# Sums of the last three output tiles of a first convolution on TensorE, 64-column sums of the input, and a new instruction order

## The chip, the cores and the metric

The kernel runs on one core of one Trainium2 chip. Time is device time in microseconds (us) for one execution; the figure to compare is the median of several executions. A profiled execution has a time of its own, and its trace spans a little less than that time.

A core has five engines that run their own instruction streams in order and wait for each other with semaphores: TensorE (PE; its weight loads are listed as PEld), VectorE (DVE), ScalarE (ACT), GpSimd (POOL) and SyncE (SP). Transfers are issued from the SP and POOL queues here.

## The reference

The input is x with 2 images of 512 channels of 64 x 64 pixels. Both convolutions are 3 x 3 with 512 output channels; group norm has 4 groups of 128 channels.

```python
h = conv3(_silu(gn(x, g1, be1)), w1)
emb = _silu(t_emb) @ w_emb
h = h + emb.reshape(B, C, 1, 1)
h = conv3(_silu(gn(h, g2, be2)), w2)
return x + h
```

The second norm needs the sum and the sum of squares of h over each group of 128 channels, which is one tile of partitions. The kernel sums the convolution's output without the embedding, and adds the embedding's part by arithmetic; a matmul with a constant matrix (line 319) then sums over the 128 partitions.

## The kernel before

**Tiling.** A chunk is half an image, 32 rows, so there are four chunks; an output tile is 128 channels of a chunk. A layer has 16 groups (chunk by output tile), numbered 0 to 15; groups 0 to 7 are image 0. The convolution uses a transform over rows, four rows to a tile, with six products ("positions"). Positions 0 and 5 are direct matmuls of 512 columns into single banks `acc` (line 934), two of which exist. The four middle positions are partly nested once more over columns and use 256-column matmuls into two-bank tiles `nst` (line 942) or `mid` (line 934).

**Inputs of the matmuls.** `activate` (line 627) applies norm and SiLU on ScalarE to one channel tile of a chunk, into `ak`; `transform` (lines 641 to 678) and `columns` (lines 558 and 563) make the planes V on VectorE. Weights R arrive by DMA and become matrices U on VectorE and ScalarE (lines 309, 308, 421, 394), in part with an accumulating transfer from the POOL queue (line 432).

**Outputs.** TensorE's banks are copied with a factor (`evac`, printed as line 308 on ScalarE or 309 on VectorE), combined on VectorE (lines 987 to 1008) and written to a ring of five buffers: three hold results `yst`, two hold a second addend `z`. For layer 0 `fin` issues an accumulating DMA from the POOL queue (line 1069) that adds z to y, and then the store of y to `h_scr` (line 1073). After that, with the next group, `sum_up` runs two passes over y on ScalarE with an accumulated output (line 795): Identity for the sum, Square for the sum of squares. `gn2_me` (lines 507 to 519) turns these into mean and mean square, and `gn2_scale` into the second norm's scale and bias.

**Sums of x.** For the first image `stats0`, for the second `gn1_stats`, use matmuls with 128 x 128 blocks of x (channels by pixels) as weights and a column of ones (`sums_pe`, line 367). Such a matmul sums over the channels and leaves 128 pixel places, over which the blocks accumulate; since the norm's group is the whole tile, the total over places is all that is needed. `gram_pe` (line 362) has the block on both sides, and its diagonal holds sums of squares.

**Order.** A table `ORDER` lists for each engine the order of its instructions, and `in_order` imposes it. `FLIP` is a string with a digit for each scaled copy, 394 in all, and says whether the copy goes to the other engine than its default (ScalarE for evacuations, VectorE for the rest).

Of the kernel before, what the change touches and what calls it, by code (L numbers as in the profile page):

```python
# [10 lines left out]
ALU = mybir.AluOpType  # L11
# [53 lines left out]
0-31 90-122 32-43 123 44-56 124 156 125 157-162 126 163-172 127-136 173-181 137-153 182-187 154-155 57-73 188 74-79  # L65
189-252 80-89 254 286 255 287-317 256-258 253 320-335 259-277 336-351 278-285 318 358 370-385 359-360 352-353
386-401 354-355 319 356-357 364-369 408-410 420-423 402-403 424-435 361-362 414 404-407 415-419 363 411-413 458 461
436-451 459 452-453 460 462-463 454 464-465 455 466 470-485 467 456-457 468-469 486-501 511-512 508 502-503 509
514-519 504-507 510 513 520-525 544-549 526-533 550 534-536 551 537 552-553 538-542 592-593 543 554-559 568 560-565
580 566-567 569-570 581-583 571-572 594 573-575 595 576 584-585 596-600 586-589 601-608 624-625 590-591 626-634 609  # L70
635-638 577-579 639-644 610-621 645 648 622-623 646-647 649-654 673 661 674 655-659 675 660 662-670 689 705-716 671
717-721 672 722-725 676 726-728 677-678 690-701 737 702-703 738 704 679-680 749-750 681-687 751-752 688 753-760
739-744 729-730 745 761 731-736 762 746 763 777 747-748 778-779 793-815 780-786 825-826 787-789 816 827 790-792 837
828 764-776 829-835 838 836 839-848 817 849 865 850-851 818 852 819-822 866-867 853-857 823 868-869 824 870-871 858
872 859 873 860-864 874-879 881 880 882-903 905-907 904 913 908 914-915 925 909 916 926 910-912 937-938 917 927-928
939-940 918 929-931 919 953 941-945 954 920 932 946 921 947-949 922 955-957 950 969 923 951-952 924 958 933-936
959-966 970-974 967-968 975 1001 976-978 1002-1004 1013 979-992 1005 1014-1015 993 1006 1016-1018 994 1025-1026
1019-1022 1027 1023 1028-1030 1007 1024 1031-1032 995-1000 1033-1036 1008-1009 1037-1038 1010-1011 1039-1040 1012
1041 1057-1058 1042 1059-1060 1043 1061 1044-1048 1062-1063 1049-1050 1064-1065 1051-1054 1066-1075 1055-1056
1076-1087 1109 1088 1097 1089 1110-1111 1090-1091 1112-1120 1125-1132 1092-1093 1141 1133 1142 1134-1136 1094 1137  # L80
1095 1138-1140 1098-1099 1121-1124 1100 1096 1101-1108 1143-1147 1157-1172 1148-1156 1173-1181 1185-1193 1182-1183
1194 1184 1195-1209 1213 1210-1212 1214-1242 1245-1260 1243 1261-1262 1285-1291 1263-1264 1244 1265-1267 1301-1302
1268-1284 1303-1315 1317-1319 1292 1316 1320-1327 1293-1295 1328-1332 1296-1300 1349-1353 1361-1362 1354-1357
1333-1348 1363 1358-1359 1373-1381 1360 1364 1382-1386 1365-1367 1387-1389 1405 1390-1394 1368-1371 1395-1404 1372
1406-1429 1437 1430-1431 1438-1441 1432-1436 1442-1443 1450-1451 1444-1448 1452-1459 1462-1463 1460-1461 1464
1478-1493 1449 1494-1495 1465-1477 1496-1502 1526-1528 1538 1529-1531 1539-1541 1510-1518 1542 1503-1509 1543
1519-1525 1532-1537 1544-1551 1566-1581 1552-1565 1582-1614 1626-1627 1615-1619 1628-1631 1638-1639 1620-1624 1632
1625 1633-1636 1654-1661 1637 1662-1670 1640-1653 1671-1701 1726-1730 1702 1731 1703 1732-1737 1704-1705 1714-1716
1706-1710 1717-1719 1711-1713 1720-1725 1742-1744 1738-1741 1745-1746 1758 1747-1749 1759-1760 1750-1757 1761-1770
1774-1777 1790-1798 1778-1785 1799 1802 1814 1771 1786-1787 1772-1773 1800 1803-1804 1788-1789 1805 1815-1816  # L90
1806-1809 1801 1810-1813 1830 1846 1831 1847 1832 1848-1853 1833 1854-1861 1834-1835 1862-1864 1817-1829 1865-1869
1836-1845 1894-1909 1870-1874 1882 1910-1912 1883-1891 1913 1926-1928 1875-1881 1929-1930 1914-1918 1892 1931-1940
1893 1919 1941-1951 1920-1925 1952-1961 1974-1985 1962-1963 1990-1992 1964 1993 1965-1967 2006-2007 1968-1969 2008
1994 2009-2012 1995-2000 1970-1971 2001-2005 2013-2015 1972-1973 2016-2025 2030-2033 2026-2028 2034-2035 1986 2036
2042-2045 2037 2046 2029 2047 1987 2048 1988-1989 2049 2038-2039 2050-2053 2040-2041 2054 2070-2071 2086 2055-2056
2087-2088 2057-2059 2089 2060-2064 2090 2072 2091 2065-2069 2073-2075 2092 2076-2077 2093 2078-2085 2094-2101 2110
2102 2111-2113 2103-2105 2123 2114 2124-2131 2115 2106-2109 2116-2117 2135-2136 2132 2137-2140 2151 2141-2145 2133
2118 2146 2167 2152 2119 2147-2149 2153 2120 2150 2134 2154-2156 2121-2122 2157-2159 2168-2171 2160-2164 2172
2165-2166 2173-2178 2183-2198 2179-2181 2199 2182 2200-2201 2211 2202-2205 2212 2223 2206-2208 2224-2226 2239-2241
2227-2231 2255-2258 2232 2259 2213 2260-2263 2242-2243 2214-2217 2209-2210 2218-2219 2244 2220-2222 2245 2233-2236  # L100
2246 2237-2238 2247-2252 2264 2253-2254 2265-2270 2287-2289 2271-2286 2290-2294 2299-2300 2311-2321 2327 2322
2328-2339 2301 2323-2326 2340-2342 2302-2303 2343-2344 2304 2295 2345 2296-2298 2305-2307 2346 2308-2310 2347-2354
2359-2372 2355-2356 2373 2357-2358 2374 2399-2414 2375-2377 2387-2396 2378-2380 2415-2421 2381-2382 2422-2423
2383-2384 2424-2426 2385-2386 2427-2430 2397-2398 2431-2446 2463-2464 2447-2462 2465-2471 2475 2487 2476 2488-2489
2477-2481 2503-2504 2482-2486 2505 2519-2521 2472-2474 2506-2509 2522-2525 2490-2502 2526 2510-2516 2527-2528
2517-2518 2529-2534 2551-2556 2535-2550 2557-2563 2575-2583 2591 2584 2564-2566 2607 2585-2587 2592 2588-2590 2608
2593 2567 2594 2568-2574 2609-2611 2595-2606 2612-2620 2623-2625 2639 2626-2628 2621-2622 2629 2640-2641 2663
2630-2631 2664-2665 2632-2635 2651 2636-2638 2666-2667 2652 2642 2668 2643-2644 2669 2653-2654 2670 2645-2646
2671-2672 2647-2648 2673-2677 2655 2678-2679 2656-2659 2680 2660 2681 2695 2682 2661 2683-2685 2662 2686-2690
2696-2701 2691-2694 2702-2704 2649-2650 2705-2726 2751-2764 2727-2728 2739 2765-2766 2740 2729-2733 2741-2742  # L110
2734-2737 2743 2767-2769 2744 2738 2770-2772 2783-2784 2773-2777 2745 2778 2746 2779-2780 2747-2748 2785-2786
# [76 lines left out]
def kernel(  # L188
# [1038 lines left out]
```

## Time and profile before

| | |
|---|---|
| median of 3 runs | 460.18 us (459.57 to 462.43) |
| profiled execution | 459.88 us |
| its span in the trace | 457.9 us |
| TensorE busy | 444.0 us (97%), 3238 matmuls |
| VectorE busy | 431.3 us (94%) |
| ScalarE busy | 386.6 us (84%) |
| GpSimd busy | 75.6 us (17%) |
| passes for sums, line 795 | 32 of 1918 ns, 61.4 us |
| one-column sums, line 367 | 224 matmuls |
| accumulating DMA, line 1069 | 28 of 512 KB, median 4.7 us from issue to landing |

Busy time of TensorE is modelled for matmuls that overlap, so the distance between starts says more than the duration of one. A wait is named by the engine whose semaphore ended it. Layer 0 ends and layer 1 begins near 220 us; some of layer 1's input work is done ahead of that.

### The profile page before, as it was taken

What the parts mean: (1) busy time and instruction counts of PE and PEld (TensorE: products, weight loads), DVE (VectorE), ACT (ScalarE), POOL (GpSimd) and SP (SyncE); (2) the same over time, 40 slices, a digit from 0 to 9 for tenths busy, and PEclk for the clock granted to TensorE, in tenths of its full rate; (3) what the DMA queues carried; (4) which work ended last, traced back from release to release, by engine and by line L of the source; (5) the groups of instructions that cost most, each with busy time, mean ns of one, the idle gap of its engine ahead of it and who ended that gap; (6) DMA issues with size and microseconds to landing.
All of it is one profiled execution on the core that took longest, in us unless ns stands there. A gap on an engine that the chain in (4) does not pass through costs nothing.

```text
span 457.9 us, 8441 instructions
## 1 busy us (share of the span) xinstructions
PE 444.0 (97%) x3238; PEld 288.2 (63%) x3238; DVE 431.3 (94%) x828; ACT 386.6 (84%) x423; POOL 75.6 (17%) x119
## 2 busy tenths in 40 slices
PE   7999999999999999997999999999999999999996
PEld 7844454556555667665656645557666666668874
DVE  2999999999999999999999999998999989999796
ACT  5899999979998798789999999647878696969761
POOL 1223301021000001210121211113221221211110
PEclk9989999999999999999899999999999999999999
DMA  8999765543846462447879895466967769637565
GB/s 311 358 385 235 155 172 146 164 129 103 190 130 159 99 180 66 120 141 212 226 164 263 217 208 125 107 139 165 211 149 184 179 163 206 137 93 151 127 155 169
DMA packets 25011, 80.05 MB, mean 175 GB/s; under 512 B 2827, under 2 KB 6027, under 8 KB 24587
## 3 DMA queue, kind: packets, MB, share of 16 engines
q0 software_dynamic: 10080, 34.87, 37.3%
q1 hardware_dynamic: 14832, 44.64, 29.4%
q8 instruction: 25, 0.41, 0.3%
q14 instruction: 15, 0.12, 0.1%
q10 hardware_dynamic: 59, 0.01, 0.0%
HBM read 42.54 MB, written 16.78 MB: 130 GB/s over the span
## 4 chain that ended last, share of the span: by engine, by line
PE 60%; DVE 19%; ACT 8%; DMA 6%; issue 6%; POOL 2%; DVEq 0%; ACTq 0%; POOLq 0%
PE nst L942 23%; PE acc L934 21%; PE mid L934 13%; ACT rm L308 2%; DVE ak L641 2%; DVE V L678 2%; ACT ak L627 2%; PE acc L1037 2%; DMA g1t<-in_w_dram 1%; DVE V L558 1%; ACT ring L795 1%; DMA out_dram<-ring 1%; DMA ring<-in_x_dram 1%; ACT ring L308 1%; PE half L934 1%
## 5 line engine op out<-in xcount | busy, mean ns | idle before, releaser
L942 PE MATMUL nst<-V,U 128*128 128x256 f16 x1600 | 210.2, 273 | 3.7 <-DVE rm L309 2.4
L942 PEld LDWEIGHTS <-U 128*128 128x128 f16 x1600 | 154.3, 97 | 55.3 <-issue 5.0
L934 PE MATMUL acc<-V,R 128*128 128x512 f16 x696 | 182.6, 384 | 1.3 <-DVE V L661 0.8
L934 PEld LDWEIGHTS <-R 128*128 128x128 bf16 x744 | 71.5, 97 | 63.5 <-issue 1.8
L308 ACT ACTIVATE rm<-nst 128x1024 f16<-128x1024 f32 x98 | 97.8, 1025 | 10.5 <-PE nst L942 4.9
L934 PE MATMUL mid<-V,U 128*128 128x512 f16 x336 | 85.3, 385 | 0.7 <-DVE U L421 0.7
L795 ACT ACTIVATE ring<-ring 128x2048 f16<-128x2048 f16 x32 | 61.4, 1918 | 1.1 <-ACT rm L308 0.7
L627 ACT ACTIVATE ak<-ak,nb_all,sc_all 128x2112 f16<-128x2112 f16 (+1 forms) x28 | 60.2, 2156 | 2.3 <-DVE nb_all L526 2.3
L934 PEld LDWEIGHTS <-U 128*128 128x128 f16 x336 | 32.4, 97 | 36.2 <-DVE U L421 1.4
L308 ACT ACTIVATE ring<-ring 128x512 f16<-128x512 f16 x58 | 35.0, 627 | 23.3 <-DVE ring L1001 16.4
L1069 POOL DMA_DIRECT2D ring<-ring x28 | 26.5, 946 | 143.6 <-ACT ring L308 122.5
L308 ACT ACTIVATE ak<-ak 128x520 f16<-128x520 f16 (+1 forms) x34 | 38.2, 1142 | 3.0 <-DVE ak L648 2.9
L641 DVE TENSOR_TENSOR ak<-ak 128x2080 f16<-128x2080 f16 x32 | 39.4, 1232 | 0.1
L678 DVE TENSOR_TENSOR V<-ak 128x1040 f16<-128x1040 f16 x54 | 38.2, 707 | 0.7 <-ACT ak L308 0.5
L989 DVE TENSOR_TENSOR rm<-tu,rm 128x1024 f16<-128x1024 f16 x50 | 34.1, 682 | 1.0 <-ACT rm L308 0.8
L563 DVE TENSOR_TENSOR V<-V 128x512 f16<-128x512 f16 (+1 forms) x62 | 34.1, 555 | 0.0
L308 ACT ACTIVATE ring<-acc 128x512 f16<-128x512 f32 x52 | 29.6, 596 | 1.8 <-DVE ring L309 0.8
L558 DVE TENSOR_TENSOR V<-V 128x1024 f16<-128x1024 f16 (+1 forms) x31 | 30.2, 978 | 0.2 <-PE acc L934 0.2
L421 DVE TENSOR_TENSOR U<-U,g1t 128x1536 f16<-128x1536 f16 x32 | 30.1, 945 | 0.0
L988 DVE TENSOR_TENSOR tu<-rm 128x512 f16<-128x512 f16 x50 | 20.8, 415 | 2.6 <-ACT rm L308 2.5
L648 DVE TENSOR_TENSOR ak<-ak 128x1040 f16<-128x1040 f16 x32 | 22.5, 702 | 0.1
L668 DVE TENSOR_TENSOR V<-ak 128x1040 f16<-128x1040 f16 x32 | 22.3, 697 | 0.0
(132 smaller groups left out, 444.9 us busy)
## 6 DMA issues: line engine op xcount, KB each, us to landing
ring<-ring POOLq DMA_DIRECT2D x28, 512.0 KB, 4.7
ak<-h_scr SPq DMA_DIRECT2D x16, 528.0 KB, 3.7
h_scr<-ring SPq DMA_DIRECT2D x16, 512.0 KB, 3.7
ring<-in_x_dram POOLq DMA_DIRECT2D x14, 512.0 KB, 5.6
out_dram<-ring POOLq DMA_DIRECT2D x14, 512.0 KB, 5.1
ak<-in_x_dram SPq DMA_DIRECT2D x12, 528.0 KB, 4.5
R<-in_w_dram SPq DMA_DIRECT2D x16, 384.0 KB, 5.2
U<-U POOLq DMA_DIRECT2D x14, 384.0 KB, 5.6
```

The lines of the kernel that those rows point to most:

```text
L308: return nc.scalar.activation(out=o, in_=i, func=ACT.Copy, scale=f)
L421: nc.vector.tensor_tensor(out=o, in0=i0, in1=i1, op=op)
L558: nc.vector.tensor_tensor(out=lo2.rearrange("p c q (t w) -> p (q t) c w", w=HALF), in0=plane_pair(0, HALF + 2), in1=plane_pair(1, HALF), o ...
L563: nc.vector.tensor_tensor(out=hi2[:, c].rearrange("p q (t w) -> p (q t) w", w=HALF), in0=i0, in1=i1, op=op)
L627: nc.scalar.activation(out=at[:, lo - r0:hi - r0, 1:W + 1], in_=sap, func=ACT.Silu, bias=nb_all[:, layer, b, ct:ct + 1], scale=sc_all[:, l ...
L641: nc.vector.tensor_tensor(out=diff, in0=diff, in1=below, op=ALU.add)
L678: nc.vector.tensor_tensor(out=o, in0=in0, in1=in1, op=op)
L795: behind(nc.scalar.activation(out=junk, in_=y, func=func, scale=scale, accum_out=acc), inst)
L934: nc.tensor.matmul(out, lhsT=w_direct(pos, ct, kx), rhs=rhs, start=first, stop=last)
L942: nc.tensor.matmul(accs["nst", (pos - 1) // 2][bank][:, q, :, plane, :], lhsT=lhsT, rhs=rhs.rearrange("p (t w) -> p t w", w=HALF), start=s ...
L989: nc.vector.tensor_tensor(out=msl[:, 1 - k:4 - k:2].rearrange("p q t w -> p q (t w)"), in0=tu[:].rearrange("p q t e w -> p q (t e w)"), in ...
L1069: add_z = lambda: nc.gpsimd.dma_start(out=flat(yst), in_=ring[:, NY + turn % NZ], accum_op=ALU.add)
```

## The change

Three parts:

- For groups 13, 14 and 15 of layer 0 the plain sums are made on TensorE. `weighted_sums` takes the 16 blocks of 128 columns of y as weights, with three columns on the other side: ones, the embedding of the second image in bf16, and what bf16 leaves of it. The result, for 128 pixel places, is the sum over channels of y and of y times the embedding; it goes into an `acc` bank and is copied to `sum_pe` by VectorE. The Identity pass of these three tiles is left out; the Square pass stays. `gn2_me` adds the weighted sums for the second image.
- `sums_pe` writes as many columns of ones as its output has: 64 for channel tiles 1 to 3 of image 0 and channel tile 0 of image 1, one for the others. One of the equal columns is read.
- All five tables of `ORDER` and the string `FLIP` are replaced. Five copies for U and one evacuation go from VectorE to ScalarE, and nine copies within the ring the other way; many others change places.

`D_BY_DMA` is false for every tile in both kernels, so the lines under it run in neither.

```diff
+    SUM_BY_PE = lambda grp: grp >= 13
...
-    FLIP = "0100100011000000000000100010010100000110...
+    FLIP = "1001101011010000000011000110000100010001...
...
-            nc.tensor.matmul(sm, lhsT=blk, rhs=ones_bf[:], start=(j == 0), stop=(j == len(blocks) - 1))
+            nc.tensor.matmul(sm, lhsT=blk, rhs=ones_bf[:].broadcast_to([P, sm.shape[1]]),
+                             start=(j == 0), stop=(j == len(blocks) - 1))
...
-        b1 = b0[:, P:P + 1]
+        b1 = b0[:, P:P + (P // 2 if ct == 0 else 1)]
...
+    def emb_columns():
+        nc.vector.memset(ones_emb[:, :, 0], 1.0)
+        nc.vector.memset(sum_pe, 0.0)
+        nc.vector.tensor_copy(out=ones_emb[:, :, 1], in_=emb_sb[:, :, B - 1])
+        nc.vector.tensor_tensor(out=ones_emb[:, :, 2], in0=emb_sb[:, :, B - 1], in1=ones_emb[:, :, 1], op=ALU.subtract)
+
+    def weighted_sums(y, ot):
+        acc = ps_acc.tile([P, NFREE], F32, tag="acc", name="sm")
+        n = y.shape[1] // P
+        for j in range(n):
+            nc.tensor.matmul(acc[:, 0:3], lhsT=y[:, j * P:(j + 1) * P], rhs=ones_emb[:, ot], start=(j == 0), stop=(j == n - 1))
+        nc.vector.tensor_copy(out=sum_pe[:, ot], in_=acc[:, 0:3])
...
+        if b == B - 1:
+            nc.vector.tensor_tensor(out=m0[:, 0], in0=sum_pe[:, :, 1], in1=sum_pe[:, :, 2], op=ALU.add)
+            for k, (part, scale) in enumerate(((sum_pe[:, :, 0], 1.0 / HW), (m0[:, 0], 2.0 / HW))):
+                nc.vector.scalar_tensor_tensor(out=me[:, k], in0=part, scalar=scale, in1=me[:, k], op0=ALU.mult, op1=ALU.add)
...
-            sums_pe(pcs, b1[:, 0:1])
+            sums_pe(pcs, b1[:, 0:P // 2])
...
-            y, junk, s1, s2 = to_sum.pop()
-            for func, scale, acc in ((ACT.Identity, 1.0, s1), (ACT.Square, float(HW) ** -0.5, s2)):
+            y, junk, s1, s2, ot = to_sum.pop()
+            if ot is not None:
+                nc.vector.memset(s1, 0.0)
+                weighted_sums(y, ot)
+            for func, scale, acc in ((ACT.Identity, 1.0, s1), (ACT.Square, float(HW) ** -0.5, s2))[ot is not None:]:
...
+                if (layer, grp) == (0, 10):
+                    emb_columns()
```

More of the change, by code (lines that the diff above doesn't have):

```diff
@@ L285 @@
         nc.gpsimd.memset(ak[:, 0:AROWS * WP].rearrange("p (r w) -> p r w", w=WP)[:, :, 0:1], 0.0)
-    gparm = consts.tile([4 * CT, P], BF16, name="gparm")
+    gp_all = consts.tile([P, P], BF16, name="gp_all")
+    gparm = gp_all[0:4 * CT]
     tparm = consts.tile([B * ET, P], BF16, name="tparm")
@@ L742, in stats0 @@
             ps_g = b1.bitcast(BF16)[:, 0:4 * CT]
-            nc.tensor.transpose(ps_g, gparm[:], ident[:4 * CT, :4 * CT])
+            nc.tensor.transpose(ps_g, gparm, ident[:4 * CT, :4 * CT])
             nc.vector.tensor_copy(out=gb[:], in_=ps_g)
@@ L1054, in ends_close, with close_group @@
                         nc.vector.tensor_tensor(out=y4[:, 0:4:3], in0=t5, in1=tt[:], op=ALU.add)
-                def close_group(layer=layer, b=b, ch=ch, ot=ot, rows=rows, turn=turn, yst=yst, y4=y4, tt=tt,
+                def close_group(layer=layer, b=b, ch=ch, ot=ot, grp=grp, rows=rows, turn=turn, yst=yst, y4=y4, tt=tt,
                                 accs=accs, by_dma=by_dma, zt=zt, by_z=by_z, ends=ends, ends_close=ends_close):
```

213 lines of the change are left out of this document (107 added, 106 removed), and 4 rows, old and new, of the table ORDER.

## The prediction

> **What bounds the kernel now.** I read the page first: busy times by slice, then the waits of TensorE.
>
> ```profile
> PE   7999999999999999997999999999999999999996
> DVE  2999999999999999999999999998999989999796
> ACT  5899999979998798789999999647878696969761
> PEclk9989999999999999999899999999999999999999
> ```
>
> ```profile
> PE nst L942 <- DVE rm L309: 2.4, 1, 2.4
> ...
> PE nst L942 <- ACT rm L308: 1.2, 3, 0.8
> ```
>
> The first four are the page's slices (40 of 11.4 us; tenths busy, and the granted clock), the last two rows of TensorE's waits (us in total, times, longest). TensorE is full but for the start, the end and one place near slice 19 (206 to 230 us), the change of layers. There VectorE and ScalarE are full too, and the clock digit falls to 8, as it does in slice 3. The table by stretches (length, then busy time and count for PE, PEld, DVE, ACT and POOL, granted clock, DMA) shows both falls:
>
> ```profile
> 18.90:22.31 3.41, 2.90 (x81) 2.72 (x78) 3.41 (x10) 3.41 (x3) 0.10 (x1) 1.00 0.99 386
> 22.31:25.72 3.41, 3.40 (x40) 2.03 (x37) 3.41 (x9) 3.41 (x6) 0.94 (x2) 0.50 0.98 325
> 25.72:47.00 21.28, 20.17 (x163) 9.85 (x161) 20.84 (x51) 20.77 (x19) 5.59 (x7) 1.00 0.98 302
> ...
> 213.46:216.87 3.41, 1.05 (x11) 0.78 (x9) 3.41 (x7) 3.41 (x4) 0.71 (x1) 1.00 0.65 115
> 216.87:220.28 3.41, 3.41 (x17) 2.43 (x17) 3.41 (x7) 2.60 (x5) 1.27 (x2) 0.50 0.61 197
> ...
> 233.00:290.00 57.00, 57.00 (x342) 32.80 (x340) 56.70 (x107) 56.01 (x61) 11.06 (x15) 1.00 0.83 195
> ```
>
> At half clock 3.41 us of matmuls cost 1.7 us more. The timelines of TensorE and of ScalarE (start, busy time, and in brackets the idle time before and who ended it) show the place closely. TensorE waits 2.36 us for an evacuation on VectorE, then 0.80 us for one on ScalarE that stands behind the two 1.9 us passes of an earlier tile's sums:
>
> ```profile
> 209.05 5.42 PE L942 MATMUL nst<-V,U 128*128 128x256 f16 x48
> 216.83 3.57 PE L942 MATMUL nst<-V,U 128*128 128x256 f16 x16 [2.36 <-DVE rm L309]
> ...
> 231.78 2.46 PE L942 MATMUL nst<-V,U 128*128 128x256 f16 x21 [0.80 <-ACT rm L308]
> ```
>
> ```profile
> 224.30 1.91 ACT L795 ACTIVATE ring<-ring 128x2048 f16<-128x2048 f16 x1
> ...
> 226.72 1.90 ACT L795 ACTIVATE ring<-ring 128x2048 f16<-128x2048 f16 x1
> ...
> 230.72 1.92 ACT L308 ACTIVATE rm<-nst 128x1024 f16<-128x1024 f32 x2
> ```
>
> **A measure.** Starts follow each other at 25 ns (1 column), 56 (128), 110 (256) and 221.5 (512) in undisturbed runs of matmuls. Pricing every matmul so gives 436.6 us of clean time: 1600 x 0.1104 + 1032 x 0.2215 = 405.2, and 31.4 for the rest. Call lag the start of a matmul less the clean time ahead of it. The last matmul ends at 453.7, so the lag ends at 17.1. It is 10.4 at the U wait before 47.02, still about 10.4 at 200, 11.3 at 201.21, and 16.3 at 231.78; only 0.8 comes later. After the last matmul 4.1 us go to the last sums and stores, and 2.0 lie around the span: 436.6 + 17.1 + 4.1 + 2.0 = 459.8, the profiled execution being 459.88. The median of the three runs is 460.18, 0.3 above it.
>
> **The change, part by part.** Added TensorE work: 48 matmuls of 3 columns, at the 25 to 27 ns of 1 and 2 columns, make 1.2 us. 128 sums go from 1 to 64 columns. No row has 64; between 25 ns and 56 ns lie +0 and +4.0 us in all. I take 28 ns, half of the 56 ns of 128 columns, since 128 to 512 columns scale so: +0.5 (3 ns x 128 = 0.4, a little more for starts). Clean time becomes 438.3, +1.7; this is paid whole wherever TensorE sets the end, which is nearly everywhere after 233.
>
> Removed: three ScalarE passes, 1.9 us each, 5.7 in all. Their passes stand now between 243 and 271 (L795 rows at 243.38, 251.25 and 266.80 begin the pairs). TensorE waits for nothing there: the row 233 to 290 has it busy 57.00 of 57.00. So by themselves they give the path nothing; they only make room after the crowded place.
>
> Front: the half clock at 22.31 follows a stretch with 63 one-column matmuls of 25 ns, in which the array streams next to nothing, and waits of 0.7 us. With 64 columns it streams nearly always, so I expect no fall there: 1.7 us on TensorE. But VectorE is busy 20.84 of the next 21.28 us, and the U that ends the wait before 47.02 is its work. In the new order VectorE has 1.8 us less before that U, and TensorE 0.8 less clean time: lag 9.4, against 10.4. ScalarE has 5 to 8 us more copies there (copies moved to it); the evacuation before clean 38.9 then ends near 48.7 to 49.5, a lag of 9.8 to 10.5. I take 10.0.
>
> Of the replaced choices, nine copies of ring rows go to VectorE (0.20 for 0.48 us) and five of U to ScalarE (0.73 for 0.27): in all ScalarE's work falls from 372.7 to 367.3 us, VectorE's stays at 423.
>
> New order at the change of layers. I count the work queued ahead of what TensorE waits for, with starts at 0.90 (rm), 0.48 (ring), 2.04 (activation L627), 1.89 (L795), 0.53 (ak), 1.37 and 0.73 (U) us. Before: from the first activation of layer 1 (196.28) to the evacuation that frees 231.78 stand 32.9 us of ScalarE work and 1.3 of waits. After: 30.7, since one activation and two copies of U and g1t are moved behind it; 1.0 of waits. The first activation itself needs the scale of layer 1, and VectorE now has 2.7 us more ahead of that chain, which waits for POOL's power (2.04 us) in between: 196.3 to 197.5, I take 197.0. ScalarE then frees TensorE at 197.0 + 30.7 + 1.0 + 0.9 = 229.6, at clean 216.2: lag 13.4.
>
> New waits behind it. TensorE loads y as weights, so it waits for the accumulating DMA (L1069 in the old lines) that completes y; the nested matmuls of layer 1 queue behind it, and ScalarE's and VectorE's evacuations wait for those. The DMA is issued about 0.5 after ScalarE's copy of the tile's last row, at 230.6. The same transfer now goes from 234.03 to 238.67, 4.6 us, the next from 243.04 to 249.95, 6.9; the 28 of this kind have a median of 4.7, and the transfers of the ring tile run from 3.0 to 8.1. With 4.6 it lands at 235.2 at clean 221.9: lag 13.3; with 8.1, 16.8. The bank of the sums is one of two `acc` banks, so the next `acc` also waits for VectorE's 3-column copy, 222.2 us of VectorE work plus 16.0 to 16.7 idle: lag 13.3 to 14.0. The second and third tiles come at clean 236.2 and 253.5, where a transfer of 4.6 to 6.5 is still covered at this lag. POOL's queue keeps the transfer ahead of two U transfers, as now; SP's keeps the store of h behind it.
>
> VectorE: the V columns needed at clean 230.5 stand behind 227.5 us of its work; with the 16.0 to 16.9 of idle it has by then, lag 13.0 to 13.9. Its 16 new small instructions (some 0.07 us each, as its 8-element rows) are in that count.
>
> The three limits agree on 13.5, against 16.3: -2.8. With +1.7: -1.1. Later waits stay at 0.8, and the end of the order (two halves, stores) is unchanged. 459.88 - 1.1 = 458.8, on the median's scale 459.1; I say 459.0. With the limits at their ends (lag 12.5 to 14.5; of the 3.5 us that the sums may cost beyond my 0.5, some 2 would lie in the front's waits of 0.8, 0.6, 0.5 and 0.45 us, so 1.5 shows) it is 457.7 to 461.2.
>
> **Rule against row.** The half clock at 216.87 followed an idle gap of 2.36 us. In the new order TensorE waits near clean 203.6 for a ScalarE copy that ends about 216.2, some 1.5 to 2.2 us, so a fall is near; before a lag of 13.4 that is fixed by ScalarE it costs little. The Trainium skill (TensorE: Matmul & The Clock Gate, Part 1 and "Why this matters for your kernels") lets the array fall to half after an idle window of about 3.4 us and asks only for gaps under some 3 us. By that rule no fall follows a 2 us gap, and rival B below would end 1.7 us earlier, at 462.0. The trace disagrees with the rule (2.36 us sufficed), so the row stands.
>
> **Rivals.**
> A, faster: the crowded place empties. VectorE's and ScalarE's idle time by 200 (16.0 and 25 to 30 us) is mostly waiting for TensorE; if the front's gain passes through it, the lag stays at 10.4. 438.3 + 10.4 + 0.8 + 6.1 = 455.6. For it: no waits at all between 47 and 200. Against: VectorE is idle 0.0 us from 200 to 233.
> B, slower: TensorE stands on the DMA of y. At a landing 5.9 us or more after the issue the lag passes 14.6 and the kernel is slower than before; with 8.1 and a half clock after that gap (1.7) the lag is 18.5: 438.3 + 18.5 + 0.8 + 6.1 = 463.7. For it: the 6.9 at 243.04, beside loads of weights. Against: median 4.7.
> C, the change doesn't do what it says: the new order wins nothing at the layers' change and the 64 columns hide behind VectorE. Lag 16.3 + 0.8, clean time 438.3: 461.5.
>
> **Numbers.** Forecast 0.44, A 0.21, B 0.21, C 0.14. Under and over 1% (4.6 us, about what can be told from no change here: 455.6 and 464.8) fall most of A's lower half and the tails of B: faster 0.17, same 0.70, slower 0.13. The range runs from just under A to just over B: 455.0 to 464.5.
>
> **What would show it.** Clock 1.00 throughout 18 to 30. 128 sums near 28 ns apart. A TensorE wait near 228 to 230 on ScalarE's evacuation, and one on the accumulating DMA in front of the 3-column matmuls; lag 13.5 behind both. No difference between 290 and the end. It is wrong if TensorE waits again after 235, if a stretch at 0.50 stands behind the new waits, or if VectorE has idle time between 200 and 230.

## The result and the profile after

| | before | after |
|---|---|---|
| median of 16 runs | 460.06 us (459.12 to 462.43) | 462.99 us (461.1 to 463.81) |
| profiled execution | 459.88 us | 462.13 us |
| its span in the trace | 457.9 us | 460.1 us |

The ratio is 1.0056, with a 95% interval of 1.0045 to 1.0067: slower by half a per cent, where 459.0 us was forecast. Two rows of the page's slices, TensorE's busy share and its granted clock:

```profile
PE   7989999999999899998989999999999999999995
...
PEclk9999999999999999999999999999999999999999
```

Both dips of the clock are gone. TensorE's row (slices of 11.5 us) has two 8s ahead of the change of layers where before has a 9: the third slice, 23 to 34 us, and the fourteenth, 150 to 161 us. TensorE's waits (us in total, times, longest) name them:

```profile
PE nst L972 <- ACT rm L313: 2.9, 4, 1.4
PE acc L964 <- ACT ring L313: 1.7, 1, 1.7
...
PE mid L964 <- DVE V L703: 1.3, 2, 1.0
PE acc L964 <- DVE V L693: 1.2, 1, 1.2
...
PE sm L524 <- DMA ring<-ring: 0.3, 1, 0.3
```

The first row holds a wait of 1.44 us that ends at 154.51 and two at the change of layers; the second ends at 218.46; the third and fourth are mainly those that end at 25.45 and 35.10; the last is the new wait of the three-column matmuls (`sm`). The stretches, with the columns of the prediction's table:

```profile
22.31:25.72 3.41, 2.36 (x47) 1.71 (x45) 2.97 (x7) 3.41 (x6) 2.18 (x2) 1.00 0.97 326
25.72:47.00 21.28, 19.49 (x155) 9.40 (x154) 20.63 (x51) 20.61 (x21) 5.23 (x7) 1.00 0.93 284
...
216.87:220.28 3.41, 1.82 (x10) 0.92 (x10) 3.41 (x7) 3.08 (x7) 0.54 (x1) 1.00 0.24 43
...
233.00:290.00 57.00, 56.71 (x378) 32.80 (x377) 56.99 (x105) 52.34 (x55) 10.90 (x15) 1.00 0.80 195
```

TensorE idles more between 22 and 47 us (19.5 busy in the second row, 20.2 before). Between 233 and 290 ScalarE has 3.7 us less work than before (52.3 against 56.0); TensorE was full there already.

**The same measure.** Clean time and lag as in the prediction, with the lag taken at the start of the matmul that stands at the given clean time (at the last matmul this counts 0.5 less than its end, which the prediction used). "After" is the time from the last matmul's start to the end of the span.

| profiled run | lag at 40 | at 200 | at 240 | last matmul | after |
|---|---|---|---|---|---|
| before | 10.3 | 11.1 | 16.1 | 16.6 | 4.6 |
| changed kernel | 10.8 | 12.9 | 16.7 | 16.4 | 5.3 |
| changed kernel, second profile | 11.5 | 13.6 | 17.4 | 17.1 | 4.6 |

Clean time went from 436.66 to 438.40. So the profiled execution grew by 1.74 (work) - 0.23 (lag) + 0.72 (after the last matmul) = 2.2 us; forecast were +1.7, -2.8 and 0. The medians differ by 2.9: the changed kernel's profiled execution is 0.9 us under its median, before's 0.2, so 0.7 us of the difference stands in neither profile. (The 1.74 prices the 64-column sums at some 29 ns. They start 30 to 32 ns apart, so about 0.3 us more is work, and is counted here as lag ahead of 40.)

The lag at 200 is 1.8 us above before's instead of under it, and this is the larger part of the question. At clean 160 the difference is even 2.9 (13.0 against 10.1): before then loses 1.0 at 201.21, by a wait for V that the new order doesn't have. The second largest part, the end, is 4.6 in the second profile: in the first, the accumulating transfer at 439.1 took 8.0 us, a store beside it 8.7, and VectorE waited 0.56 us for the load behind them; in the second they took 5.5 and 6.2.

The forecast was that ScalarE starts the first activation of layer 1 at 197.0 and frees TensorE at 229.6. Before's first activation, then the changed kernel's, and the matmul that it frees:

```profile
196.28 2.15 ACT L627 ACTIVATE ak<-ak,nb_all,sc_all 128x2112 f16<-128x2112 f16 x1 [2.32 <-DVE nb_all L526]
```

```profile
198.98 2.15 ACT L650 ACTIVATE ak<-ak,nb_all,sc_all 128x2112 f16<-128x2112 f16 x1
```

```profile
232.51 6.01 PE L972 MATMUL nst<-V,U 128*128 128x256 f16 x52 [1.02 <-ACT rm L313]
```

TensorE is freed at 232.51, at clean 216.2: a lag of 16.3 where 13.4 was forecast. Of these 2.9 us, 2.0 are the late first activation, and 0.9 the way from it to TensorE, which took 33.5 us instead of 32.6.

The stall that ends at 154.51 (TensorE's last start ahead of it is at 152.8), seen from TensorE and from ScalarE (start, busy time, idle time before and who ended it):

```profile
154.51 2.35 PE L972 MATMUL nst<-V,U 128*128 128x256 f16 x20 [1.44 <-ACT rm L313]
```

```profile
143.20 1.02 ACT L313 ACTIVATE rm<-mid 128x1024 f16<-128x1024 f32 x1 [0.62 <-PE mid L964]
146.05 1.91 ACT L823 ACTIVATE ring<-ring 128x2048 f16<-128x2048 f16 x1 [1.82 <-DMA ring<-ring]
```

The sum pass at 146.05 waited 1.82 us for the accumulating DMA that completes its tile; the evacuation TensorE needs stands behind both of the tile's passes (the second starts at 148.49). The transfers issued between 139 and 147 us (KB, us to landing):

```profile
ak<-in_x_dram SPq DMA_DIRECT2D x1, 528.0 KB
ring<-ring POOLq DMA_DIRECT2D x1, 512.0 KB, 6.4
```

The new order has SP issue a load of x at 140.11, beside the accumulating DMA of 139.50, which took 6.4 us. In before the same tile's DMA went from 137.47 to 141.91, 4.4 us, with no packets of other transfers beside its own, and its pass came 1.8 us after the landing.

### The profile page after: what moved, and what is told of

The parts are those of the page before. It is cut to its first block, busy times and chain, and to the rows that moved or that the text cites. A ratio compares the mean times of both kernels' runs of the same rounds, so it can differ in the third digit from the quotient of the medians.

```text
span 460.1 us, 8539 instructions
## 1 busy us (share of the span) xinstructions
PE 443.9 (96%) x3286; PEld 288.4 (63%) x3286; DVE 432.0 (94%) x844; ACT 383.8 (83%) x414; POOL 73.7 (16%) x119
## 4 chain that ended last, share of the span: by engine, by line
PE 39%; DVE 26%; DMA 14%; ACT 10%; issue 7%; POOL 2%; ACTq 0%; DVEq 0%; SPq 0%; POOLq 0%
PE nst L972 17%; PE acc L964 14%; PE mid L964 7%; ACT rm L313 3%; ACT ak L650 3%; DMA out_dram<-ring 3%; DVE ak L666 3%; DMA ring<-ring 3%; DMA ring<-in_x_dram 2%; DVE V L581 2%; DVE V L586 2%; DVE rm L1019 2%; DVE V L703 2%; DMA U<-U 2%; DMA g1t<-in_w_dram 2%
## 5 line engine op out<-in xcount | busy, mean ns | idle before, releaser
L972 PE MATMUL nst<-V,U 128*128 128x256 f16 x1600 | 203.9, 271 | 2.9 <-ACT rm L313 2.9
L964 PE MATMUL acc<-V,R 128*128 128x512 f16 x696 | 178.7, 383 | 2.9 <-ACT ring L313 1.7
L964 PE MATMUL mid<-V,U 128*128 128x512 f16 x336 | 83.9, 384 | 1.8 <-DVE V L703 1.3
L823 ACT ACTIVATE ring<-ring 128x2048 f16<-128x2048 f16 x29 | 55.4, 1910 | 6.6 <-issue 3.2
L313 ACT ACTIVATE ring<-ring 128x512 f16<-128x512 f16 x49 | 29.5, 625 | 21.2 <-DVE ring L1031 12.6
L1099 POOL DMA_DIRECT2D ring<-ring x28 | 24.4, 871 | 139.3 <-ACT ring L313 114.8
L703 DVE TENSOR_TENSOR V<-ak 128x1040 f16<-128x1040 f16 x54 | 38.7, 717 | 0.1
L1017 DVE TENSOR_TENSOR tu<-rm 128x512 f16<-128x512 f16 x50 | 21.3, 425 | 3.0 <-ACT rm L313 2.9
L313 ACT ACTIVATE U<-R 128x768 f16<-128x768 bf16 (+1 forms) x22 | 23.6, 1102 | 0.2
L1018 DVE TENSOR_TENSOR tu<-rm 128x512 f16<-128x512 f16 x50 | 21.3, 426 | 2.2 <-ACT rm L313 2.2
```

What stands on the lines that cost most here:

```text
L313: return nc.scalar.activation(out=o, in_=i, func=ACT.Copy, scale=f)
L703: nc.vector.tensor_tensor(out=o, in0=in0, in1=in1, op=op)
L823: behind(nc.scalar.activation(out=junk, in_=y, func=func, scale=scale, accum_out=acc), inst)
L964: nc.tensor.matmul(out, lhsT=w_direct(pos, ct, kx), rhs=rhs, start=first, stop=last)
L972: nc.tensor.matmul(accs["nst", (pos - 1) // 2][bank][:, q, :, plane, :], lhsT=lhsT, rhs=rhs.rearrange("p (t w) -> p t w", w=HALF), start=s ...
L1099: add_z = lambda: nc.gpsimd.dma_start(out=flat(yst), in_=ring[:, NY + turn % NZ], accum_op=ALU.add)
```

## The experiments

Each ratio is to the kernel before, run beside it. Kernels that leave work out say so in their expectation.

### The parts of the change

**64 columns in the old order** (e3):

```diff
-            nc.tensor.matmul(sm, lhsT=blk, rhs=ones_bf[:], ...
+            nc.tensor.matmul(sm, lhsT=blk, rhs=ones_bf[:].broadcast_to([P, sm.shape[1]]), ...
-        b1 = b0[:, P:P + 1]
+        b1 = b0[:, P:P + (P // 2 if ct == 0 else 1)]
-            sums_pe(pcs, b1[:, 0:1])
+            sums_pe(pcs, b1[:, 0:P // 2])
```

> The kernel before with 64 columns for the sums of x, order unchanged. Theory: clean time +0.5 to +0.7, no granted clock under 0.9 between 18 and 30, VectorE's U still ends the wait before 47, so the lag there is 9.9 to 10.4 and the median 459.9 to 460.5. Rival (the clock's 1.7 us are won whole): lag 9.2 or less, median 458.9 or less. Second rival (64 columns cost more): median over 461.

Measured: 459.77 us, ratio 0.9993 (0.9982 to 1.0005), lag at 40 of 9.6 and at the last matmul of 16.45. The stretch where before fell to half clock:

```profile
22.31:25.72 3.41, 3.16 (x58) 2.15 (x55) 3.41 (x10) 3.41 (x6) 0.88 (x1) 1.00 0.99 325
```

The fall is gone, VectorE is still full; by 240 us the lag is down by 0.6 to 0.7, about what the columns added in work, and the time doesn't change. The theory holds for the time; the lag of 9.6 lies between its 9.9 and the rival's 9.2. One profile doesn't settle that: e6, in which nothing is changed at the front, has 9.7. Nor is the fall itself certain in the old order. Of its three profiles with one column, before fell at 22.31 and e6 at 21.41, while e11 fell at 7.50, in a wait for the first loads, and not here; the two with 64 columns (e3 and e10) didn't fall here.

**One column in the new order** (e2; in the changed kernel the second and third edits of this diff undone):

> The changed kernel with the sums of x back at 1 column, order unchanged. Theory (64 columns cost 0.5 us of TensorE and save a half clock that VectorE hides): clean time -0.5, granted clock 0.50 in one 3.4 us stretch between 18 and 30 again, lag behind the wait before 47 between 10.6 and 11.4, median 462.5 to 463.2. Rival (the half clock is paid whole): lag +1.2 to +1.7 all the way, median 464.0 to 464.5. Second rival (the 64 columns cost more than their starts show): median under 462.2.

Measured: 462.39 us, 1.0051 (1.0029 to 1.0073); lag at 40 of 10.9. No stretch under full clock there: this execution doesn't fall even with one column. The second profile of the changed kernel, with 64 columns, does, one window later:

```profile
22.49:25.90 3.41, 2.13 (x44) 1.54 (x42) 2.97 (x7) 3.41 (x6) 2.18 (x2) 1.00 1.01 331
25.90:29.32 3.42, 3.42 (x20) 1.64 (x20) 2.81 (x11) 3.42 (x6) 0.00 (x0) 0.50 1.01 383
```

Ahead of it is a 1.06 us wait for a V column at 25.88; the first profile has the same wait, 1.03 us, and didn't fall. Of the eleven profiles of the new order with 64 columns four fell at the front (this one, e1 at 27.01, e4 at 25.73, e14 at 25.16). So in the new order 64 columns don't prevent the fall, and whether one column brings it more often a single profile can't tell. The forecast return of the half clock was a miss, and the time tells no difference.

**What the removed passes were worth in the old order** (e6; e11 has `11 <= n_summed[0] <= 13` in the same place):

```diff
-            for func, scale, acc in ((ACT.Identity, 1.0, s1), ...
+            few = P if n_summed[0] > 13 else y.shape[1]
+            for func, scale, acc, n in ((ACT.Identity, 1.0, s1, few), ...
```

> The kernel before with the plain sums of the last three tiles of layer 0 taken over 128 of their 2048 columns on ScalarE (5.1 us less of ScalarE, nothing else): what removing the passes is worth in the old order. Theory (as predicted: TensorE waits for nothing between 233 and 290 in it, the passes lie beside other work): median within 0.4 us of the kernel before, lag behind 290 at 16.0. Rival (ScalarE is the bound there although TensorE shows no wait): lag behind 290 under 15.5, median 458.0 to 459.5.

> The kernel before with the plain sums of three tiles over 128 of 2048 columns, as in e6, but of the three tiles whose passes stand at 198.33, 208.25 and 224.30 instead of the last three: the same 5.1 us taken from ScalarE inside the crowded place instead of behind it. Theory (ScalarE's queue there sets the lag, VectorE stands close behind it): TensorE's wait on ScalarE at 231.78 is gone, lag behind 233 13.5 to 15.2 instead of 16.0, median 458.2 to 459.4. Rival (VectorE alone sets it): lag 15.8 to 16.2, median within 0.4 us of the kernel before.

Measured: 1.0004 (0.9987 to 1.0022) and 1.0007 (0.9989 to 1.0024). Taken behind the crowded place or inside it, the 4.8 us less of ScalarE (three passes of 0.3 instead of 1.9) bring nothing that these intervals could show, some 1 us at most. (e6's lag behind 290 is 15.3, as its rival had it, but it was 0.6 lower than before's already at 40; from 200 to 240 it grew by 4.8.) For e11 the waits say why:

```profile
PE nst L945 <- DVE rm L309: 2.9, 1, 2.9
```

The wait on ScalarE at 231.78 is gone, but the one on VectorE's evacuation is 2.9 us instead of 2.4 in this profile, and from 200 to 240 the lag grows by 4.8 (before 5.0). VectorE's queue gives the same lag as ScalarE's: e11's rival. (Its lag itself, 16.6, is above both ranges, because this execution came to 40 with 11.5.)

**The passes back on ScalarE in the new order** (e4): `SUM_BY_PE` false for every group, the 48 matmuls and their copies taken out of the tables, an Identity pass put ahead of each Square pass.

> The changed kernel, its order kept, with the plain sums of the three last tiles back on ScalarE (each Identity pass right ahead of its Square pass) and without the 48 three-column matmuls. Theory (the matmuls are paid whole and the passes lie beside other work): clean time -1.2, no wait of TensorE on the accumulating DMA near 238, median 461.6 to 462.1. Rival (the new order needs the 5.7 us of ScalarE that it has won after 233): TensorE waits for evacuations on ScalarE between 240 and 290, lag there over 17.5, median 464 to 467.

Measured: 465.82 us, 1.0134 (1.0111 to 1.0156). The rival holds. From TensorE's timeline:

```profile
246.22 2.90 PE L970 MATMUL nst<-V,U 128*128 128x256 f16 x25 [1.11 <-ACT rm L311]
...
266.00 2.13 PE L970 MATMUL nst<-V,U 128*128 128x256 f16 x18 [1.70 <-ACT rm L311]
```

The new order has used the freed room; with the passes in it, it is 1.34% slower than the old order, without them 0.56%. The part of the change that a reader would suspect, the matmuls in place of the passes, is the one that pays in this order. What costs must then be the order (and the added work): that is by elimination, since no run takes the rest of the order back.

**The matmuls themselves** (e7; `n = 1` in `weighted_sums`):

> The changed kernel with the three-column matmuls of the first 128 of 2048 columns alone for each of the three tiles (3 matmuls instead of 48; the waits for the accumulating DMAs and for the accumulator's bank stay): what the 45 matmuls themselves cost. Theory (25 ns each, paid whole): clean time -1.1, lag unchanged (16.2 to 16.8 behind 240), median 1.0 to 1.3 us under the changed kernel. Rival (they hide in waits that come anyway, or drain): lag higher by as much, median within 0.4 us of the changed kernel. Second rival (they cost more, by what stands behind them): 2 us or more.

Measured: 462.42 us, 1.0049 (1.0032 to 1.0065), against 462.73 and 1.0065 (1.0047 to 1.0082) of the changed kernel beside it. Spans of the profiles: 458.9 and 460.1. Their difference fits 25 ns each, but the two profiles' lags at 40, 10.4 and 11.5, differ by as much; and the difference of the medians, 0.3, is too uncertain to hold for or against it.

### The stall at 152.8

**e1** was meant to put the load of x behind the store of h, but exchanged that store with a load of weights:

```diff
-... 68 71 56 52 73 57 53 ...
+... 68 71 56 73 52 57 53 ...
```

> Only SP's order is changed: the load of x into ak issued at 140.11 goes behind the store of h that waits for the accumulating DMA of 139.50, so that the two no longer run side by side. Theory (the earlier stall moved the change of layers): the accumulating DMA takes 4.4 to 4.9 us instead of 6.4, ScalarE's sum pass at 146.05 starts some 1.8 us earlier, TensorE's wait of 1.44 us at 154.51 is gone, the lag stays near 11.5 up to 200 instead of 13.0, ScalarE's first activation of layer 1 starts near 197.2 instead of 198.98, the lag behind 233 is 14.5 to 15.0 instead of 16.3, and the median falls by 1.2 to 2.0 us, to about 461.4. Rival (the new order is limited at the change of layers by its own work): the stall at 154 goes, but the lag behind 233 is 16 again and the median stays within 0.4 us of 463.0.

Measured: 461.87 us, 1.0043 (1.0022 to 1.0064); accumulating DMA 6.4 us, stall 1.42 us, as in the changed kernel. It says nothing on the theory, but is one more profile: 4.7 us after the last matmul.

**e5** exchanges the right pair:

```diff
-... 68 71 56 52 73 57 53 ...
+... 68 71 52 56 73 57 53 ...
```

> In the run e1 the exchanged pair was the store of h and a load of weights, not the pair that was meant. Here the load of x into ak (140.11 in the changed kernel) goes behind the store of h, which waits for the accumulating DMA of 139.50, so that they no longer run side by side. Theory (the stall at 152.8 is the load's doing and carries on to the end): the accumulating DMA takes 4.4 to 4.9 us instead of 6.4, TensorE's wait of 1.44 us at 154.51 shrinks under 0.3, the lag between 160 and 200 is 11.3 to 11.9 instead of 13.0, ScalarE's first activation of layer 1 starts some 1.5 us earlier than 198.98, the lag behind 240 is 14.8 to 15.6 instead of 16.7 and the median 461.0 to 462.0. Rival (the change of layers takes it back): lag 13 or less at 200 but 16.3 or more behind 240, median 462.5 to 463.2. Second rival (ScalarE is late there anyway): the wait at 154 stays over 1 us though the transfer is short.

The transfers between 139 and 147 us, ScalarE's timeline, and TensorE's row in place of the stalled one:

```profile
ak<-in_x_dram SPq DMA_DIRECT2D x1, 528.0 KB, 4.5
ring<-ring POOLq DMA_DIRECT2D x1, 512.0 KB, 4.4
```

```profile
148.92 2.15 ACT L650 ACTIVATE ak<-ak,nb_all,sc_all 128x2112 f16<-128x2112 bf16 x1 [0.55 <-DMA ak<-in_x_dram]
...
197.63 2.15 ACT L650 ACTIVATE ak<-ak,nb_all,sc_all 128x2112 f16<-128x2112 f16 x1
```

```profile
149.36 6.06 PE L972 MATMUL nst<-V,U 128*128 128x256 f16 x51
```

In the profile the theory holds step by step: 4.4 us, TensorE's wait gone from the timeline (0.3 us left between starts), lag 11.5 at 200 and 15.2 at 240, first activation of layer 1 at 197.63 instead of 198.98, span 458.8. The time doesn't follow: 462.61 us (460.8 to 465.22), 1.0074 (1.0051 to 1.0097), and the profiled execution was the fastest of six. So the collision causes the stall, and the stall was carried to the end in this execution, but something else varies between executions.

**e8** removes the stall in another way, and **after_again** is the changed kernel beside e5 to e7.

```diff
+    FEW = 7
...
+            n = P if n_summed[0] == FEW else y.shape[1]
...
-                behind(nc.scalar.activation(out=junk, in_=y, ...
+                behind(nc.scalar.activation(out=junk[:, 0:n], in_=y[:, 0:n], ...
```

> The changed kernel with ScalarE's two sum passes at 146.05 and 148.49 (one tile's) over 128 of 2048 columns; order unchanged, the two transfers still side by side. It takes the stall at 152.8 away in another way than e5: ScalarE still waits for the accumulating DMA, but is 3.4 us shorter behind it. Theory (that stall is carried through the change of layers to the end): wait at 154 under 0.3, lag at 200 11.3 to 11.9, lag behind 240 14.9 to 15.6, median 461.3 to 462.0, ratio to before 1.0025 to 1.0045. Rival (what is won there is lost at the change of layers): lag behind 240 at 16.4 or more, ratio 1.005 to 1.007.

> The changed kernel itself beside these three: a second profile of it. Theory: the stall at 152.8 and the waits at 216 and 231 are in the order and come again within 0.2 us; the 8.0 us of the accumulating transfer at 439.1, and with it 0.6 us of the 0.72 that the end of the kernel took longer, is that one execution's, as 5.5 us of the same transfer in the run e1 speaks for; median 462.6 to 463.3.

after_again: 462.73 us; the stalls at 153, 217 and 232 come again (1.76, 1.85 and 1.5 us between starts against 1.60, 1.86 and 1.5), the end takes 4.6. e8: 461.98 us, 1.0041 (1.0023 to 1.0058); lag at 200 of 11.3, but 16.7 at 240. The ratio lies in the theory's range and the lag at 240 in the rival's. In this execution what was won was lost again, at the places TensorE's timeline shows:

```profile
230.17 0.38 PE L976 MATMUL nst<-V,U 128*128 128x256 f16 x2 [0.69 <-ACT rm L313]
...
238.79 0.16 PE L524 MATMUL sm<-gp_all,ring 128*128 128x3 bf16 x1 [1.21 <-DMA ring<-ring]
```

The same two rows of the changed kernel:

```profile
231.11 0.38 PE L972 MATMUL nst<-V,U 128*128 128x256 f16 x2 [0.16 <-ACT rm L313]
...
238.81 0.16 PE L524 MATMUL sm<-gp_all,ring 128*128 128x3 bf16 x1 [0.29 <-DMA ring<-ring]
```

Both differences go back to accumulating DMAs. Issue to landing of the two concerned, and the time from landing to the first use, from the records of the traces:

| accumulating DMA near | 139 us | 219 us | 233 us |
|---|---|---|---|
| before: transfer; landing to first use | 4.4; 1.83 | 5.1; 0.77 | 4.6; 4.71 |
| changed kernel | 6.4; 0.16 | 4.8; 0.02 | 5.3; 0.14 |
| second profile of it | 6.5; 0.16 | 4.7; 0.02 | 5.3; 0.13 |
| e1 | 6.4; 0.16 | 5.1; 0.02 | 5.4; 0.14 |
| e7 | 6.6; 0.16 | 5.1; 0.02 | 5.4; 0.14 |
| e2 | 6.8; 0.16 | 5.9; 0.02 | 6.3; 0.13 |
| e5 | 4.4; 0.18 | 4.7; 0.02 | 5.3; 0.13 |
| e8 | 6.4; 0.07 | 5.6; 0.02 | 6.2; 0.13 |
| e9 | 4.4; 0.18 | 5.5; 0.02 | 6.2; 0.14 |

In before the first use came 0.8 to 4.7 us after the landing. (In e6, also the old order, the transfer near 219 took 5.7 us and the first use came 0.09 us after it, still without a wait.) In the new order it comes 0.02 to 0.18 us after it: the user stands ready, and whatever the transfer takes beyond its shortest time goes on the path. The idle time of ScalarE ahead of its pass behind the transfer near 219 shows this: 0.00 to 0.05 us where the transfer took 4.7 to 4.8 us, 0.4 with 5.1, 0.8 and 0.9 with 5.5 and 5.6, 1.2 with 5.9. The same transfers, in the same order of issue, took up to 1.2 us longer in some executions than in others, and the lag between 200 and 240 grows with them: by 3.7 to 3.8 with the short ones (both profiles of the changed kernel, e5), by 4.0 and 4.2 with those between (e1, e7) and by 5.2 to 5.7 with the long ones (e8, e9, e2; e8's passes at 146 still start 0.07 us after the landing, but they are short).

### The three exposed transfers

A transfer is called exposed here when its first user already stands ready as it lands.

**e9**: e5's exchange, and two scale steps of VectorE (`sc_all`, line 340) moved behind the V columns after them.

> The changed kernel with e5's exchange (load of x behind the store of h) and, on VectorE, the two scale steps that stand in POOL's power at 24.61 (0.44 us idle) and 31.29 (0.17) moved behind the V columns and copies that follow them. Theory: front lag 0.3 to 0.5 under the changed kernel's (10.83 and 11.52 in two profiles), no stall at 152.8, lag behind 240 14.4 to 15.2, median 461.0 to 461.8. Rival (the spread between executions, which e5 showed, comes from the moved load: it now ends next to ScalarE's activation, which it held up by 0.55 us in the profile): the median is no lower than the changed kernel's, and a profile of a slow execution shows ScalarE waiting over 1 us for the load of x near 148.

Measured: 463.28 us, 1.0062 (1.0042 to 1.0082); front lag 11.1, so no gain of VectorE's steps shows. The rival holds, and e5's exchange is seen to trade one late transfer for another:

```profile
149.86 2.15 ACT L650 ACTIVATE ak<-ak,nb_all,sc_all 128x2112 f16<-128x2112 bf16 x1 [1.09 <-DMA ak<-in_x_dram]
```

The moved load took 5.0 us here (4.5 in e5), and 0.86 us of the stall at 153 is back. The transfers at 219 and 233 took 5.5 and 6.2.

**e12 and e13** cover the waits at the change of layers: ten nested matmuls of TensorE ahead of the three-column ones, and in e13 the Identity pass at 224 short as well.

```diff
-... 1702 1718 1703-1708 1719 1709-1710 ...
+... 1780-1789 1702 1718 1703-1708 1719 1709-1710 ...
```

> As e5, and ten nested matmuls (1.1 us) that TensorE does after the first tile's three-column matmuls now stand ahead of them, so that the accumulating DMA has 1.1 us more to land. Theory (first use stands 0.02 to 0.16 us behind the landing of the accumulating DMA at the tiles of 146, 224 and 238 us, so that every longer transfer is paid; two of the three stay exposed in e5): TensorE's wait of 0.43 to 1.43 us in front of the three-column matmuls is under 0.3, the lag behind 245 is 14.6 to 15.0 where the transfer at 219 takes 4.7 us, 15.2 to 15.9 where it takes 5.5 or more, and the ratio to before is 1.002 to 1.0045. Rival (the accumulators behind come late instead): lag as in e5 for the same transfer (15.2 or 16.7), ratio 1.005 or more.

> As e12, and ScalarE's plain-sum pass at 224.5 over 128 of 2048 columns, which gives it 1.7 us behind the accumulating DMA of 219: none of the three transfers is exposed any more. Theory: lag behind 245 14.2 to 15.0 in whatever execution is profiled, ratio to before 1.000 to 1.003, spread of the times narrower than e5's 4.4 us. Rival (the transfers' length doesn't matter, the scatter comes from the front): lag at 200 and lag behind 245 differ by 4 or more as in e8, ratio 1.004 or more.

e12: 461.96 us, 1.0048 (1.003 to 1.0066), just above its range and with an interval that holds the rival's too. TensorE's wait before `sm` is gone, the lag falls to 15.2 at clean 230, and a wait of 0.55 us for ScalarE's evacuation at 247 takes it back to 15.9. e13: 461.41 us, 1.0026 (1.0015 to 1.0038), runs within 1.7 us (e5: 4.4). The time is as the theory said, and so is the spread, though spreads say little here: the runs of before beside e14 range over 4.0 us. The lag at 240, 16.0, is above its 14.2 to 15.0. ScalarE's timeline shows what stands next:

```profile
226.95 1.48 ACT L312 ACTIVATE U<-R 128x1536 f16<-128x1536 bf16 x1 [0.75 <-DMA R<-in_w_dram]
229.11 1.02 ACT L312 ACTIVATE rm<-nst 128x1024 f16<-128x1024 f32 x1 [0.68 <-DVE ring L1033]
```

With the pass short, ScalarE waits for a load of weights, then for VectorE, and frees TensorE hardly earlier: the limits here do lie close together.

**e14**: the three covered without e5's exchange (e8's passes, e13's pass, e12's ten matmuls).

> The changed kernel in SP's own order, with the three places covered that stand right behind an accumulating DMA, and without e5's exchange (whose moved load held ScalarE up by 0.55 to 1.09 us in e5, e9 and e12): both sum passes at 146 and the plain-sum pass at 224 over 128 of 2048 columns (as e8 and e13), ten nested matmuls ahead of the three-column ones (as e12). Theory (these three waits and the 1.74 us of TensorE work are what the changed kernel loses): no stall over 0.2 us at 153, lag at 200 11.0 to 11.6, lag behind 250 15.0 to 15.6, ratio to before 1.001 to 1.003, spread of the times under 2.5 us. Rival (something else moves between executions): lag behind 250 minus lag at 200 over 4.6, ratio 1.004 or more.

Measured: 460.82 us, 1.0025 (1.0011 to 1.0039), runs from 460.3 to 461.72. No stall at 153, the lag grew by 4.0 from 200 to 240, and the spread is 1.4 us. The lags themselves, 12.7 and 16.7, miss the ranges, because this execution had a half clock at the front (25.16 to 28.57 us; lag of 11.9 at 40). The ratio is under the changed kernel's interval. The difference, 0.0056 - 0.0025 = 0.31%, is 1.4 us, by the two intervals together some 0.6 to 2.3; it is what the three exposed waits account for, if nothing else in e14 helps. A rival is left: ScalarE also has 4.8 us less work in e14. e6 and e11 found no gain from that in the old order; in the new one it wasn't priced by itself. What is left to before, 0.25% or 1.15 us, is less than the 1.74 us of added work.

### A try at a faster kernel

**e10**: before with 64 columns, VectorE's evacuation of 215.57 ahead of one V column, two evacuations of ScalarE ahead of copies of U and g1t.

> The kernel before with 64 columns (as e3), and two moves at the change of layers: VectorE's evacuation of 215.57 ahead of one V column (214.74), ScalarE's evacuations of 230.72 and 231.63 ahead of the copies of U and g1t at 228.62 and 229.99. Theory (ScalarE's queue from the first activation of layer 1 sets the lag behind 231): TensorE's wait at 216.83 shrinks from 2.36 to 1.5 us, the wait at 231.78 ends about 1 us earlier, lag behind 233 14.6 to 15.2 instead of 15.5 in e3, median 458.7 to 459.6. Rival (U comes late and TensorE waits for it near 240): lag behind 250 over 15.6, median 460 or more.

Measured: 461.22 us, 1.0034 (1.002 to 1.0047): slower. Waits and stretches:

```profile
PE nst L943 <- ACT rm L308: 2.8, 3, 2.3
PE nst L943 <- DVE rm L309: 1.7, 1, 1.7
```

```profile
228.19:231.60 3.41, 1.12 (x11) 0.85 (x9) 3.41 (x9) 1.71 (x2) 0.00 (x0) 1.00 0.64 188
231.60:235.01 3.41, 3.41 (x18) 2.37 (x17) 3.41 (x7) 3.41 (x6) 0.15 (x1) 0.50 0.15 49
```

VectorE's wait shrank (2.4 to 1.7, planned 1.5) and its half clock went, but TensorE then ran into ScalarE 2.3 us long, and the half clock followed there. Lag (16.7 behind 250) and time are the rival's, though TensorE waited for an evacuation and not for U. No kernel tried beats before by more than the measurement tells.

## Why the prediction was wrong, point by point

- **The step that failed is the lag behind the layer change, 16.3 to 13.5.** It is built on the first activation of layer 1 ("196.3 to 197.5, I take 197.0") and on a front lag of 10.0 that I took straight to the change of layers. The activation came at 198.98, the lag at 200 was 12.9, and TensorE was freed at a lag of 16.3 where 13.4 was forecast. The anchor accounts for 2.0 of these 2.9 us. The sum over ScalarE's queue accounts for 0.9: 33.5 us from the activation to TensorE's start instead of 32.6, and the same in e5 (197.63 to 231.08). It counts the right instructions, but they took 31.6 us from start to start instead of 30.7. The wait of TensorE at clean 203.6 came as forecast (1.70 us, ended at 218.46).
- **Where the anchor slipped.** I read "no waits at all between 47 and 200" off the old trace and let the new order keep it. The stall at 152.8 (1.6 us of lag) is a wait of ScalarE on the accumulating DMA beside a load of x. e5 shows the collision as its cause (6.4 to 4.4 us) and e5 and e8 that without it the lag at 200 is 11.3 to 11.5 and the first activation comes at 197.6 and 197.5, next to the forecast 196.3 to 197.5. So the stall is 1.4 of the anchor's 2.0 us. The medians don't show the stall by itself: e5 has 1.0074, and e8 1.0041 with an interval that holds the changed kernel's 1.0056. I had weighed landing times only for y behind 230, not for the same transfer at the other tiles, though the old trace has all of their landings and the orders give each first use.
- **The front, 10.4 to 10.0, failed too.** Twelve profiles of the new order have 10.4 to 12.0 at clean 40, on average 11.0, five of the old order 9.6 to 11.6, on average 10.2. I followed the U before 47 alone; the new waits are for V columns at 25 and 35. Which of VectorE's steps costs this stays open: e9's two moves brought nothing that shows.
- **The fall to half clock at 22.31, removed by 64 columns and hidden by VectorE.** That VectorE hides it is right for the old order (e3). That the columns remove it is in keeping with the old order's five profiles (two of three with one column fell there, neither of the two with 64), but not with the new order's, four of which fell at the front with 64 columns. The stretch ahead of the fall held 57 one-column matmuls, not 63, among its 81.
- **The three passes, which "by themselves" give the path nothing**: in the old order e6 shows no gain. In the new order e4, which has them in place of the 1.2 us of matmuls, is 2.8 us above the changed kernel by the medians and 3.6 by the two ratios: that order has filled the room. A part's price holds for the order it is measured in.
- **The added 1.7 us of TensorE work**: 1.74 as priced; but the 64-column sums mostly start 30 to 32 ns apart, not 28, which makes 0.8 us of them instead of 0.5 and about 2.0 in all. Whether it is paid whole no run shows: e7 can't tell, and e14 is 1.15 us above before with all of it.
- **The wait on the DMA of y (rival B).** The mechanism is there, but small: 0.3 us with a transfer of 5.3 and 1.2 with 6.2 to 6.3, where B had one of 8.1 and a half clock, 5 us together. The measured 463.0 lies next to B's 463.7 by chance: this wait brings only a part of it. C's lag of 16.3 at the change of layers came about, though not because the new order won nothing there (the lag grew by 3.8, before by 5.0), but because it had lost 1.8 us ahead of it.
- **The end, unchanged**: not always. Seven of the twelve profiles of the new order have 4.6 to 4.7 us after the last matmul's start, the second profile of the changed kernel among them; the other five (the first profile, e5, e9, e12, e13) have 5.1 to 5.3. The five of the old order all have 4.6. VectorE's wait for a load explains the first profile's 5.3 in the main and 0.2 us of e12's; in e5, e9 and e13 VectorE ends as early as elsewhere, and the 0.4 us come behind it, where only the last stores are left. Why the new order has it was not found.
- **Half clock at the change of layers.** The old trace fell after a gap of 2.36 us and I kept that row against the rule of the Trainium skill (TensorE: Matmul & The Clock Gate, Part 1), which asks for an idle window of about 3.4 us. e10 fell after 2.29 us, in a window with TensorE 1.12 of 3.41 us busy; the waits of 1.7 to 1.8 us that end near 218 (1.82 of 3.41 busy in the changed kernel) were followed by none in twelve profiles of the new order. So at the change of layers gaps well under the rule's suffice, and 1.8 us does not. The length of a gap alone doesn't decide: at the front the second profile of the changed kernel fell after 1.06 us, with 2.13 of 3.41 us busy ahead of the fall.

## What to carry to other kernels

A new order has to be checked for the distance from each transfer's landing to its first use, not only for work per engine: an order that puts users right behind the landings of short transfers pays for every longer one, while one that leaves 0.8 to 4.7 us between the two, as before does, hides it. A transfer that is issued beside another lands late (here after 6.3 to 6.8 us instead of 4.4), so a load that isn't urgent belongs behind the one that someone waits for, if its own user leaves room. And one profile is one execution: e5's was its fastest of six.

## What the runs showed of the hardware

- The accumulating DMA of 512 KB near 140 us took 4.4 us where the load of x was issued near its end or behind it (before and the other four profiles of the old order, e5, e9, e12, e13) and 6.3 to 6.8 us with that load of 528 KB issued 0.6 us after it (the changed kernel twice, e1, e2, e4, e7, e8, e14). The Trainium skill (DMA: Bandwidth & Descriptors, "Queues, rings and completion order") has each DMA engine take turns between the queues that have work; the two durations agree with that.
- At 219 and 233 us the same transfers with the same neighbours took 4.7 to 4.8 and 5.3 us in some executions of the new order, 5.1 and 5.4 in others and 5.5 to 5.9 and 6.2 to 6.3 in others again, long or short together. What decides between them was not found.
